# One scheduling region, warm-up matmuls, and row statistics moved from GpSimd to VectorE, in a fused attention, Fourier and feed-forward kernel

## The chip, the cores and the metric

The kernel runs on 1 core of one Trainium2 chip. The metric is device time in microseconds (us) of one execution. The kernel before took 933.96 us, the median of 3 runs (933.89 to 934.87).

## The reference

```python
# q, k, v: (4, 12, 448, 64)    w_ch1: (768, 3072)    w_ch2: (3072, 768)
scores = cap * np.tanh(scale * (q @ k.T) / cap)          # cap = 30
attn = exp(scores - max); attn = attn / (sum(attn) + 1e-9)
x = heads_to_columns(attn @ v)                            # (4, 448, 768)
mixed = np.real(fft(fft(x, axis=1), axis=2))
u = x + mixed
un = (u - mean(u)) / np.sqrt(var(u) + 1e-6)               # over the 768 features
return u + np.maximum(un @ w_ch1, 0) @ w_ch2
```

## The kernel before, in words

Five engines work from one list of steps. A step is a small function (`scores`, `tanh`, `exp`, `weigh`, `normalise`, ...) that issues a few instructions on one or two engines; the table `ORDER` gives every step its place, the list `plan` is sorted by it, and `run` issues it. Each engine takes its instructions strictly in the order in which they were issued to it, and waits at the first whose operands are not ready.

**Attention.** The 12 heads of the 4 batches are 24 pairs of heads; a query block has 84 score tiles. For a tile, TensorE makes the scores (`s`, L378), ScalarE does tanh (L388) and exp (L391) over 900 columns, and TensorE multiplies the weights with the values (`weigh`, tile `av`, L407, 7 units for each pair of heads). The sum `av` of a pair has one PSUM buffer. VectorE divides it by its denominators (`denominators`, L422 and L423; `normalise`, L429) into `u`, and only then can TensorE begin `weigh` of the next pair. The scores have two PSUM buffers.

**Transform of a batch**, once its six pairs are done: folds on VectorE (`fold_tokens` L448, `mirror` L454, `fold_features` L463 to L467), a small matmul (`stage1`, tile `yps`, L479), `combine` (L499), a second matmul (`stage2`, tile `pq`, L507), and its addition to `u` on VectorE (`add_u`, L527 and L531). `moments` (L540, L541) makes mean and variance of each token. `rows` makes from them the inverse deviation `r` by a power and one Newton step, in ten tiny operations of GpSimd (L549 to L558). `rows_cols` and `rows_copy` turn mean and deviation into rows, four small transfers (`rows_out`) put these into DRAM, and `row` reads them back, broadcast to all partitions. `standardise` (L584, VectorE) applies scale and bias to the four blocks of `u` of a batch; `u_cols` (L591, TensorE) transposes them, `u_copy` (ScalarE) takes them to SBUF, `operand` and `operand_rest` (through the helpers L299 on ScalarE and L304 on VectorE) split them into a high and a low part, and `residual` (L715, VectorE) turns the copy back into `u` for the final sum.

**Feed-forward.** w_ch1 and w_ch2 are cut into 12 groups. For each group and batch, `up` (tile `ph`, L725) makes two blocks of 128 hidden units in 36 matmuls of 448 columns, with relu on ScalarE (L736) and the low part on VectorE (L737); `down` (tile `po`, L759) adds 36 matmuls into the output, with an addition on VectorE for every six of them (L767). A `product` step is six of these matmuls. The first group goes in the order U0 D0 U1 D1 U2 D2 U3 D3 (U for `up`, D for `down`, the digit is the batch) and is mixed with the transform of the last batch. The `weights` steps convert weights on VectorE and ScalarE (L638 to L672).

**Two regions.** `run` opens a scheduling region each time that it is called. It is called for the steps up to the last `tanh`, with two double PSUM banks for scores, and again for the rest, with four banks for `up`.

```python
cut = 1 + max(i for i, x in enumerate(plan) if x[2][0] == "tanh")
with tc.tile_pool(name="psum_s", bufs=2, space=PSUM) as stage["scores"]:
    run(plan[:cut])
stage["up"] = ctx.enter_context(tc.tile_pool(name="psum_f", bufs=4, space=PSUM))
run(plan[cut:])
```

At the start, `load_cap` brings `cap`, and `scales` (L325 to L332) makes from it `tscale`, which tanh needs, and then `guard` with an exp on ScalarE, which only the denominators need.

Of the kernel before, what the change touches and what calls it, by code (L numbers as in the profile page):

```python
# [11 lines left out]
F32 = mybir.dt.float32  # L12
# [4 lines left out]
ALU = mybir.AluOpType  # L17
# [86 lines left out]
    "exp": [  # L104
# [4 lines left out]
    ],  # L109
    "fetch": [  # L110
        24, 71, 106, 128, 205, 214, 257, 360, 412, 835, 873, 899, 900, 952
    ],
    "fold_features": [
        211, 212, 193, 202, 419, 438, 402, 405, 641, 648, 630, 642, 822, 825, 820, 821
    ],
    "fold_tokens": [
        67, 68, 163, 137, 187, 200, 261, 345, 397, 401, 399, 394, 456, 463, 627, 636, 626, 633, 673, 684, 806,
        757, 813, 810
    ],
    "load_cap": [  # L120
        4
    ],
    "load_constant": [
        228, 144, 251, 39
    ],
    "load_k": [
        1, 22, 43, 74, 100, 124, 135, 182, 153, 206, 270, 289, 319, 357, 425, 428, 450, 467, 527, 532, 634, 676,
        713, 685
    ],
    "load_q": [  # L130
        2, 10, 12, 42, 69, 50, 95, 73, 107, 127, 174, 157, 183, 242, 244, 274, 262, 312, 342, 366, 370, 395,
        461, 430, 465, 466, 503, 535, 596, 584, 603, 678, 679, 719, 747, 711
    ],
    "load_v": [
        11, 27, 31, 46, 78, 77, 80, 98, 114, 115, 133, 143, 156, 196, 194, 210, 246, 263, 265, 266, 299, 287,
        351, 344, 373, 359, 381, 388, 426, 433, 475, 501, 519, 509, 560, 547, 604, 576, 619, 644, 691, 703, 733,
        731, 759, 741, 784, 782
    ],
    "mirror": [
        188, 201, 400, 404, 628, 639, 814, 817  # L140
    ],
    "moments": [
        283, 295, 302, 306, 482, 498, 508, 510, 727, 729, 755, 728, 853, 855, 856, 854
    ],
    "normalise": [
        47, 65, 104, 126, 162, 184, 209, 255, 286, 315, 341, 390, 435, 455, 495, 536, 567, 592, 640, 672, 722,
        752, 775, 809
    ],
    "operand": [
        643, 384, 574, 416, 474, 523, 646, 777, 647, 723, 689, 824, 807, 818, 880, 913, 919, 915, 941, 940, 924,  # L150
        935, 907, 926
    ],
    "operand_rest": [
        655, 470, 575, 564, 477, 582, 651, 798, 761, 730, 769, 826, 836, 872, 894, 914, 920, 916, 943, 942, 949,
        936, 922, 928
    ],
    "product": [
        811, 812, 827, 828, 829, 841, 848, 851, 852, 861, 862, 863, 864, 865, 871, 875, 879, 885, 901, 908, 909,
        927, 929, 930, 931, 932, 933, 934, 937, 938, 946, 947, 948, 959, 960, 962, 963, 964, 965, 966, 967, 968,
        970, 972, 973, 980, 981, 982  # L160
    ],
    "residual": [
        656, 686, 665, 594, 702, 778, 896, 840, 763, 735, 772, 888, 918, 912, 910, 951, 956, 961, 944, 969, 950,
        974, 945, 953
    ],
    "row": [
        588, 734, 867, 939
    ],
    "rows": [
        327, 545, 768, 870  # L170
    ],
    "rows_cols": [
        343, 563, 779, 876
    ],
    "rows_copy": [
        356, 566, 781, 877
    ],
# [88 lines left out]
def attention_fft_ffn(  # L266
# [53 lines left out]

    def load_cap():
        nc.sync.dma_start(capt, cap.partition_broadcast(P))

    def scales():
        nc.vector.reciprocal(tscale, capt)  # L325
        nc.vector.tensor_scalar_mul(tscale, tscale, 1.0 / math.sqrt(D))


        nc.vector.tensor_scalar_mul(ncap, capt, -1.0)
        nc.vector.tensor_tensor(ncap, ncap, capt, op=ALU.min)  # L330
        nc.scalar.activation(guard, ncap, AF.Exp)
        nc.vector.tensor_scalar_mul(guard, guard, 1e-9)  # L332
# [482 lines left out]
    for i in range(4):  # L815
        at(load_constant, i)
# [173 lines left out]
```

## Time and profile before

| what | value |
|---|---|
| median of 3 runs | 933.96 us |
| the profiled execution's own time | 934.84 us |
| its span, first to last instruction | 932.7 us |
| TensorE busy | 914.1 us (98%) |
| VectorE busy | 715.8 us (77%) |
| ScalarE busy | 326.1 us (35%) |
| GpSimd busy | 16.7 us (2%) |
| TensorE clock granted, mean | 0.998 |

The span is 2.1 us shorter than the execution. In the rows, PE is TensorE's matmuls, PEld its weight loads, DVE is VectorE, ACT ScalarE, POOL GpSimd and SP the queue that issues most transfers. TensorE's busy share is near 98%, so a loss of time on it is seen either as the short idle times in brackets, or as matmuls that take longer than others of the same shape.

### The profile page before, as it was taken

The numbers are of one execution on the slowest core, as the hardware profiler recorded it, in microseconds if no ns is written. First come the engines' busy times: TensorE is split into PE (matmuls) and PEld (weight loads), VectorE is DVE, ScalarE is ACT, GpSimd is POOL, SyncE is SP. The second block draws the span as 40 slices with busy tenths as digits, with TensorE's granted clock in tenths as the row PEclk, the third lists the DMA queues.
The fourth block names the chain that finished last, engine by engine and source line by source line (L and its number), as shares of the span: only waits on it lengthen the run. The fifth ranks groups of instructions, "written<-read, shape, count | busy, mean of one in ns | idle before, by whom it ended". The sixth has DMA issues, their size and how long they took to land.

```text
span 932.7 us, 18658 instructions
## 1 busy us (share of the span) xinstructions
PE 914.1 (98%) x7822; PEld 790.5 (85%) x7822; DVE 715.8 (77%) x1447; ACT 326.1 (35%) x499; POOL 16.7 (2%) x47
## 2 busy tenths in 40 slices
PE   8999999989999999999999999999999999999998
PEld 4666776668889999999998999999999999999997
DVE  2689698879989787878878778777777778777633
ACT  7989989861312222122121221212122221122100
POOL 0001010010100000000000000000000000000000
PEclk9999999999999999999999999999999999999999
DMA  6654435210202121221212121211122111121033
GB/s 184 172 152 134 131 89 130 65 38 1 79 0 85 52 61 51 61 66 54 61 51 61 52 62 47 62 51 51 52 58 62 51 51 51 52 68 51 18 114 123
DMA packets 50611, 66.63 MB, mean 71 GB/s; under 512 B 25568, under 2 KB 36704, under 8 KB 50528
## 3 DMA queue, kind: packets, MB, share of 16 engines
q1 hardware_dynamic: 50240, 65.12, 24.3%
q8 instruction: 61, 1.00, 0.4%
q10 hardware_dynamic: 288, 0.33, 0.1%
q14 instruction: 22, 0.18, 0.1%
HBM read 59.91 MB, written 5.52 MB: 70 GB/s over the span
## 4 chain that ended last, share of the span: by engine, by line
PE 87%; ACT 7%; DVE 4%; issue 1%; POOL 1%; DMA 0%; POOLq 0%; DVEq 0%
PE po L759 37%; PE ph L725 36%; PE av L407 6%; PE s L378 5%; ACT a L391 3%; ACT a L388 3%; PE yps L479 1%; PE pq L507 1%; PE pt L591 1%; DVE xc L715 1%; DVE xc L767 0%; DVE bs L540 0%; DMA q<-qr 0%; POOL ln L551 0%; DVE hh L737 0%
## 5 line engine op out<-in xcount | busy, mean ns | idle before, releaser
L759 PE MATMUL po<-hh,w 128*128 128x448 f32 x1734 | 362.4, 366 | 2.0 <-DVE xc L767 1.6
L725 PE MATMUL ph<-xs,w 128*128 128x448 f32 x1728 | 360.1, 367 | 0.0
L759 PEld LDWEIGHTS po<-hh,w 128*128 128x128 f32 x1734 | 323.1, 188 | 34.0 <-DVE xc L767 4.6
L725 PEld LDWEIGHTS ph<-xs,w 128*128 128x128 f32 x1728 | 324.2, 188 | 28.5 <-issue 0.4
L767 DVE TENSOR_TENSOR xc<-xc,po 128x448 f32<-128x448 f32 x289 | 176.4, 616 | 42.6 <-PE po L759 42.2
L737 DVE SCALAR_TENSOR_TENSOR hh<-ph,hh 128x448 fp32r<-128x448 f32 x96 | 59.9, 624 | 97.0 <-ACT hh L736 96.9
L638 ACT ACTIVATE wt<-raw 128x384 f32<-128x384 f32 x84 | 46.6, 554 | 231.1 <-DVE w L672 231.1
L736 ACT ACTIVATE hh<-ph 128x448 fp32r<-128x448 f32 x96 | 52.3, 545 | 191.8 <-PE ph L725 191.8
L407 PEld LDWEIGHTS av<-vt,a 128*64 128x64 f32 (+3 forms) x3072 | 87.2, 132 | 31.3 <-issue 20.3
L407 PE MATMUL av<-vt,a 128*64 128x65 f32 (+3 forms) x3072 | 93.2, 224 | 4.9 <-issue 4.3
L388 ACT ACTIVATE a<-s,tscale 128x900 f32<-128x900 f32 x84 | 82.7, 1003 | 10.3 <-PE s L378 9.8
L391 ACT ACTIVATE a<-a,capt 128x900 f32<-128x900 f32 x84 | 85.3, 1043 | 1.4
L299 ACT CAST w<-wt 128x384 fp32r<-128x384 f32 x84 | 42.8, 510 | 119.1 <-DVE wt L647 119.1
L378 PE MATMUL s<-q,k 64*64 64x450 f32 x672 | 78.9, 571 | 5.4 <-DMA q<-qr 4.4
L647 DVE SCALAR_TENSOR_TENSOR wt<-wt 128x384 f32<-128x384 f32 x96 | 53.6, 558 | 9.6 <-DVE wt L644 0.5
L644 DVE SCALAR_TENSOR_TENSOR wt<-raw,wt 128x384 uint32<-128x384 uint32 x96 | 53.6, 559 | 3.3
L672 DVE TENSOR_TENSOR w<-wt 128x384 fp32r<-128x384 f32 x96 | 53.6, 558 | 3.3
L666 DVE SCALAR_TENSOR_TENSOR wt<-raw,wt 128x384 f32<-128x384 uint32 x96 | 53.5, 558 | 2.9
L304 DVE TENSOR_TENSOR wt<-wt,w 128x384 f32<-128x384 f32 x96 | 52.8, 550 | 0.0
L378 PEld LDWEIGHTS s<-q,k 64*64 64x64 f32 x672 | 20.6, 136 | 27.2 <-ACT a L388 11.4
L641 DVE TENSOR_SCALAR wt<-raw 128x384 uint32<-128x384 uint32 x96 | 34.1, 355 | 1.1
L663 DVE TENSOR_SCALAR wt<-wt 128x384 uint32<-128x384 uint32 x96 | 34.0, 354 | 0.6
(58 smaller groups left out, 324.0 us busy)
## 6 DMA issues: line engine op xcount, KB each, us to landing
raw<-w2r SPq DMA_DIRECT2D x48, 384.0 KB, 3.9
raw<-w1r SPq DMA_DIRECT2D x48, 384.0 KB, 3.0
q<-qr SPq DMA_DIRECT2D x35, 225.0 KB, 3.9
outT<-xc SPq DMA_DIRECT2D x23, 224.0 KB, 1.9
k<-kr SPq DMA_DIRECT2D x12, 256.0 KB, 3.3
vt<-vr SPq DMA_DIRECT2D x24, 128.0 KB, 4.6
k<-kr SPq DMA_DIRECT2D x12, 192.0 KB, 2.5
vt<-vr SPq DMA_DIRECT2D x24, 96.0 KB, 4.1
```

The source lines that it names most:

```text
L378: nc.tensor.matmul(ps_t[t][h * D : (h + 1) * D, n, :SQ], kt[q, k][rows, k0, h], qk[q, x][rows], start=True, stop=True,)
L388: nc.scalar.activation(a_t[t], ps_t.pop(t)[:, :, :SQ], AF.Tanh, scale=tscale)
L391: nc.scalar.activation(a_t[t], a_t[t], AF.Exp, scale=capt)
L407: nc.tensor.matmul(pa_t[p][q0:q1, j, g * (D + 1) : (g + 1) * (D + 1)], a_t[t][rows, n, OFF[g] + q0 : OFF[g] + q1], vt[rows, p % 2, i], sta ...
L644: nc.vector.scalar_tensor_tensor(tu, hi.bitcast(U32), 0xC0000000, tu, op0=ALU.bitwise_and, op1=ALU.bitwise_or)
L647: nc.vector.scalar_tensor_tensor(t, w, HI_MIN, t, op0=ALU.is_ge, op1=mul)
L666: nc.vector.scalar_tensor_tensor(w, lo, 2.0**-52, w, op0=mul, op1=mul)
L672: nc.vector.tensor_tensor(ws[c][1][:, sl], t, w, op=add)
L725: nc.tensor.matmul(ph[:, :S], w_[:, dc * P : (dc + 1) * P], x_, start=(k_ == 0), stop=(k_ == 3 * NDC - 1),)
L737: nc.vector.scalar_tensor_tensor(hh[:, 1], ph[:, :S], 0.0, f32(hh[:, 0]), op0=ALU.max, op1=sub)
L759: nc.tensor.matmul(po[:, q0:q1], w_[:, dc * P : (dc + 1) * P], hh[:, x_, q0:q1], start=(k_ == 0), stop=(k_ == 3 * GF - 1),)
L767: nc.vector.tensor_tensor(ac[:, q0:q1], ac[:, q0:q1], po[:, q0:q1], op=add)
```

## The change

All steps are issued in one region. Seven matmuls of the identity matrix with itself stand first on TensorE (`warmup`). `scales` now only makes `tscale`; the rest of it is a step of its own (`guards`) behind the second tanh. Of the ten operations of `rows`, the addition and the power stay on GpSimd; six on VectorE take the place of the other eight. The transposed rows come straight from `stat`. `standardise` of the last batch goes to ScalarE. The table has new numbers throughout; two lines of it show their form.

```diff
     "denominators": [
-        45, 64, 97, 123, 161, 178, 208, 254, 284, 314, 335, 389, 434, 454, 494, 530, 565, 591, 638, 670, 715,
-        751, 774, 808
+        50, 65, 98, 124, 162, 186, 211, 255, 289, 314, 342, 383, 434, 456, 502, 539, 564, 596, 639, 671, 727,
+        755, 775, 805
...
+    def warmup():
+        warm = psum.tile([P, 512], F32, tag="d", name="warm")
+        for _ in range(7):
+            nc.tensor.matmul(warm[:, :P], ident, ident, start=True, stop=True)
+
...
     def scales():
         nc.vector.reciprocal(tscale, capt)
         nc.vector.tensor_scalar_mul(tscale, tscale, 1.0 / math.sqrt(D))
+
+    def guards():
...
     def rows(b):
-        ln = line[b] = new([P, 2, 4, 2], F32, "ln", 2, "ln")
-        var = new([P, 4], F32, "var", 1, "var")
+        ln = line[b] = new([P, 4, 2], F32, "ln", 2, "ln")
         t = new([P, 4], F32, "nt", 1, "nt")
-        nc.gpsimd.tensor_copy(ln[:, 0, :, 0], stat[b][:, :, 0])
-        nc.gpsimd.tensor_scalar_add(var, stat[b][:, :, 1], 1e-6)
-        nc.gpsimd.tensor_tensor(ln[:, 1, :, 0], var, mhalf, op=ALU.pow)
-        nc.gpsimd.tensor_tensor(t, ln[:, 1, :, 0], ln[:, 1, :, 0], op=mul)
-        nc.gpsimd.tensor_tensor(t, t, var, op=mul)
-        nc.gpsimd.tensor_scalar(t, t, -0.5, 1.5, op0=mul, op1=add)
-        nc.gpsimd.tensor_tensor(ln[:, 1, :, 0], ln[:, 1, :, 0], t, op=mul)
-        nc.gpsimd.tensor_tensor(ln[:, 0, :, 1], ln[:, 1, :, 0], var, op=mul)
-        nc.gpsimd.tensor_tensor(t, ln[:, 0, :, 0], ln[:, 1, :, 0], op=mul)
-        nc.gpsimd.tensor_scalar_mul(ln[:, 1, :, 1], t, -1.0)
+        n = new([P, 4], F32, "var", 1, "var")
+        mean, var, r = stat[b][:, :, 0], stat[b][:, :, 1], ln[:, :, 0]
+        nc.gpsimd.tensor_scalar_add(t, var, 1e-6)
+        nc.gpsimd.tensor_tensor(r, t, mhalf, op=ALU.pow)
+        nc.vector.tensor_tensor(n, t, r, op=mul)
+        nc.vector.tensor_tensor(n, n, r, op=mul)
+        nc.vector.tensor_scalar(n, n, -0.5, 1.5, op0=mul, op1=add)
+        nc.vector.tensor_tensor(r, r, n, op=mul)
+        nc.vector.scalar_tensor_tensor(ln[:, :, 1], mean, -1.0, r, op0=mul, op1=mul)
+        nc.vector.tensor_tensor(var, t, r, op=mul)
...
-            ps[:8, :R], line[b][:R, 0].rearrange("q g a -> q (g a)"), ident[:R, :R], start=True, stop=True
+            ps[:8, :R], stat[b][:R].rearrange("q g a -> q (g a)"), ident[:R, :R], start=True, stop=True
...
-        scale, bias = ln[:R, 1, g, :1], ln[:R, 1, g, 1:]
-        nc.vector.tensor_scalar(u, u, scale, bias, op0=mul, op1=add)
+        scale, bias = ln[:R, g, :1], ln[:R, g, 1:]
+        if b == B - 1:
+            nc.scalar.activation(u, u, AF.Identity, bias=bias, scale=scale)
+        else:
+            nc.vector.tensor_scalar(u, u, scale, bias, op0=mul, op1=add)
...
     def run(steps):
-        with tc.manual_schedule():
-            for _, _, key, f, args, needs in steps:
...
+        for _, _, key, f, args, needs in steps:
...
-    with tc.tile_pool(name="psum_s", bufs=2, space=PSUM) as stage["scores"]:
-        run(plan[:cut])
-    stage["up"] = ctx.enter_context(tc.tile_pool(name="psum_f", bufs=4, space=PSUM))
-    run(plan[cut:])
+    with tc.manual_schedule():
+        with tc.tile_pool(name="psum_s", bufs=2, space=PSUM) as stage["scores"]:
+            run(plan[:cut])
+        stage["up"] = ctx.enter_context(tc.tile_pool(name="psum_f", bufs=4, space=PSUM))
+        run(plan[cut:])
```

What the changes do to the order of the instructions is shown at three places. Line numbers after the change are 6 to 15 higher than before.

VectorE where pair 22, the last but one, is divided; `den` are the denominators, L584 is `standardise` of batch 2, L448 a fold, `xs` an `operand_rest`, L715 a `residual`. Before:

```order
L541 BN_AGGR stat<-bs 113x2
L448 TENSOR_TENSOR tf<-u 113x4x128
L304 TENSOR_TENSOR xs<-xc,xs 128x448
L715 TENSOR_TENSOR xc<-xc,dev 128x448
L304 TENSOR_TENSOR xs<-xc,xs 128x448 x2
L715 TENSOR_TENSOR xc<-xc,dev 128x448
L584 TENSOR_SCALAR u<-u,ln 113x768 x2
L448 TENSOR_TENSOR tf<-u 113x4x128
L422 TENSOR_SCALAR den<-av,guard 113x8
L423 RECIPROCAL den<-den 113x8
L429 TENSOR_TENSOR u<-av,den 113x4x128
```

and after the change, from the same `moments` on (L554 is the former L541):

```order
L554 BN_AGGR stat<-bs 113x2
L461 TENSOR_TENSOR tf<-u 113x4x128
L310 TENSOR_TENSOR xs<-xc,xs 128x448
L728 TENSOR_TENSOR xc<-xc,dev 128x448
L563 TENSOR_TENSOR var<-nt,ln 128x4
L564 TENSOR_TENSOR var<-var,ln 128x4
L565 TENSOR_SCALAR var<-var 128x4
L566 TENSOR_TENSOR ln<-ln,var 128x4
L567 SCALAR_TENSOR_TENSOR ln<-stat,ln 128x4
L568 TENSOR_TENSOR stat<-nt,ln 128x4
L435 TENSOR_SCALAR den<-av,guard 113x8
L436 RECIPROCAL den<-den 113x8
```

Before, two `standardise`, a fold and two `operand_rest` with a `residual` stand between the `moments` and the denominators of pair 22, although the table has the denominators (774) ahead of both `standardise` (780 and 785) and of one `operand_rest` (798): the two regions had moved four instructions forward. After, they stand behind the division, and the six new tiny operations stand ahead of it.

ScalarE at the start of the program; `guard<-ncap` is the exp of `guards`, L388 (now L401) is tanh, L391 (now L404) is exp. Before:

```order
L311 ACTIVATE guard<-mhalf 128x1
L331 ACTIVATE guard<-ncap 128x1
L388 ACTIVATE a<-s,tscale 128x900 x2
L391 ACTIVATE a<-a,capt 128x900 x2
L388 ACTIVATE a<-s,tscale 128x900
```

After:

```order
L317 ACTIVATE guard<-mhalf 128x1
L401 ACTIVATE a<-s,tscale 128x900 x2
L344 ACTIVATE guard<-ncap 128x1
L404 ACTIVATE a<-a,capt 128x900 x2
L401 ACTIVATE a<-s,tscale 128x900
```

The guard's exp has moved from ahead of the first two tanh to behind them.

VectorE in the transform of the last batch; L527 and L531 (now L540 and L544) are the additions of `stage2`, each group of four belonging to one product in PSUM, and L767 (now L780) is the addition behind a `down` product. Before:

```order
L737 SCALAR_TENSOR_TENSOR hh<-ph,hh 128x448
L527 TENSOR_TENSOR u<-u,pq 113x2x384 x4
L531 TENSOR_TENSOR u<-u,pq 113x384 x4
L767 TENSOR_TENSOR xc<-xc,po 128x448
L531 TENSOR_TENSOR u<-u,pq 113x384 x4
L767 TENSOR_TENSOR xc<-xc,po 128x448 x2
```

After:

```order
L750 SCALAR_TENSOR_TENSOR hh<-ph,hh 128x448
L540 TENSOR_TENSOR u<-u,pq 113x2x384 x4
L544 TENSOR_TENSOR u<-u,pq 113x384 x8
L780 TENSOR_TENSOR xc<-xc,po 128x448 x2
L550 MEMSET stat 128x8
```

The `down` product that stood between the third and the fourth `stage2` now follows the fourth.

## Rows read from the trace of the kernel before

**Rows 1.** The page's first part: busy time and share by engine.
```profile
PE 914.1 (98%) x7822; PEld 790.5 (85%) x7822; DVE 715.8 (77%) x1447; ACT 326.1 (35%) x499; POOL 16.7 (2%) x47
```

**Rows 2.** Stages: length; busy us of PE, PEld, DVE, ACT, POOL; clock; DMA share, GB/s.
```profile
10.00:60.00 50.00, 49.00 (x1149) 31.31 (x1143) 30.81 (x71) 49.38 (x53) 0.00 (x0) 1.00 0.62 175
60.00:187.00 127.00, 125.00 (x2726) 89.05 (x2724) 106.94 (x237) 112.44 (x138) 7.74 (x20) 1.00 0.40 109
187.00:204.00 17.00, 12.91 (x306) 10.31 (x301) 11.34 (x25) 10.41 (x14) 4.15 (x10) 0.90 0.15 39
204.00:282.00 78.00, 73.98 (x460) 64.27 (x459) 72.21 (x149) 18.72 (x40) 4.06 (x10) 1.00 0.10 28
282.00:932.00 650.00, 647.64 (x3174) 593.97 (x3172) 493.02 (x960) 130.31 (x254) 0.00 (x0) 1.00 0.20 60
```

**Rows 3.** Timeline, 0 to 9 us: start, duration, engine, line, operation, idle before.
```profile
4.43 6.24 PE L378 MATMUL s<-q,k 64*64 64x450 f32 x32 [4.43 <-DMA q<-qr]
5.89 0.15 DVE L326 TENSOR_SCALAR tscale<-tscale 128x1 f32<-128x1 f32 x1
6.39 0.20 ACT L331 ACTIVATE guard<-ncap 128x1 f32<-128x1 f32 x1 [3.73 <-DVE ncap L330]
6.50 0.99 ACT L388 ACTIVATE a<-s,tscale 128x900 f32<-128x900 f32 x1
7.78 1.01 ACT L388 ACTIVATE a<-s,tscale 128x900 f32<-128x900 f32 x1 [0.28 <-PE s L378]
```

**Rows 4.** Score matmuls as a group, 0 to 14, then 140 to 190 us.
```profile
L378 PE MATMUL s<-q,k 64*64 64x450 f32 x40 | 7.2, 872 | 4.4 <-DMA q<-qr 4.4
...
L378 PE MATMUL s<-q,k 64*64 64x450 f32 x176 | 19.9, 552 | 0.0
```

**Rows 5.** Stages of 1 us, columns as in rows 2.
```profile
5.00:6.00 1.00, 1.00 (x11) 0.25 (x6) 0.28 (x3) 0.00 (x0) 0.00 (x0) 1.00 0.80 232
...
200.00:201.00 1.00, 1.00 (x24) 1.00 (x23) 0.00 (x0) 0.00 (x0) 0.00 (x0) 0.50 0.47 56
```

**Rows 6.** Timeline, 188 to 204 us, around the division of pair 22.
```profile
188.97 3.63 PE L407 MATMUL av<-vt,a 128*64 128x65 f32 x128
189.57 0.21 DVE L541 BATCH_NORM_AGGREGATE stat<-bs 113x2 f32<-113x12 f32 x1
191.03 1.39 POOL L551 TENSOR_TENSOR ln<-var,mhalf 128x4 f32<-128x4 f32 x1
192.71 0.62 DVE L715 TENSOR_TENSOR xc<-xc,dev 128x448 f32<-128x448 f32 x1
194.74 1.27 DVE L584 TENSOR_SCALAR u<-u,ln 113x768 f32<-113x768 f32 x2 [1.41 <-POOL ln L558]
196.53 0.22 DVE L422 TENSOR_SCALAR den<-av,guard 113x8 f32<-113x8 f32 x1
197.02 0.69 DVE L429 TENSOR_TENSOR u<-av,den 113x512 f32<-113x512 f32 x1
197.81 5.17 PE L407 MATMUL av<-vt,a 64*64 64x65 f32 x128 [3.17 <-issue]
203.03 0.23 DVE L422 TENSOR_SCALAR den<-av,guard 113x8 f32<-113x8 f32 x1 [3.44 <-PE av L407]
```

**Rows 7.** Timeline, 210 to 224 us, transform of the last batch on TensorE.
```profile
210.83 1.78 PE L479 MATMUL yps<-seqT,ff 112*64 112x113 f32 x32
...
216.42 2.18 PE L507 MATMUL pq<-featT,y 97*64 97x192 f32 x32
...
220.73 1.48 PE L759 MATMUL po<-hh,w 128*128 128x448 f32 x6
222.14 1.20 PE L507 MATMUL pq<-featT,y 97*64 97x192 f32 x16
```

**Rows 8.** VectorE's groups by shape, whole span: busy us, mean ns of one.
```profile
L527 DVE TENSOR_TENSOR u<-u,pq 113x768 f32<-113x768 f32 x16 | 14.3, 942 | 0.7 <-PE pq L507 0.7
L584 DVE TENSOR_SCALAR u<-u,ln 113x768 f32<-113x768 f32 x16 | 10.1, 671 | 2.1 <-POOL ln L558 2.0
L423 DVE RECIPROCAL den<-den 113x8 f32<-113x8 f32 x24 | 4.9, 203 | 0.8
```

More of the change, by code (lines that the diff above doesn't have):

```diff
@@ L115 @@
     ],
     "fold_tokens": [
-        67, 68, 163, 137, 187, 200, 261, 345, 397, 401, 399, 394, 456, 463, 627, 636, 626, 633, 673, 684, 806,
-        757, 813, 810
+        67, 68, 167, 137, 191, 204, 257, 347, 392, 401, 393, 391, 459, 470, 630, 641, 598, 600, 674, 691, 804,
+        763, 808, 809
+    ],
+    "guards": [
+        11
     ],
     "load_cap": [
-        4
+        5
     ],
     "load_constant": [
-        228, 144, 251, 39
+        233, 139, 217, 116
     ],
     "load_k": [
-        1, 22, 43, 74, 100, 124, 135, 182, 153, 206, 270, 289, 319, 357, 425, 428, 450, 467, 527, 532, 634, 676,
@@ L128 @@
-        713, 685
+        2, 30, 42, 75, 100, 90, 144, 184, 168, 213, 270, 320, 285, 366, 423, 428, 455, 469, 530, 546, 612, 678,
+        634, 720
     ],
     "load_q": [
-        2, 10, 12, 42, 69, 50, 95, 73, 107, 127, 174, 157, 183, 242, 244, 274, 262, 312, 342, 366, 370, 395,
-        461, 430, 465, 466, 503, 535, 596, 584, 603, 678, 679, 719, 747, 711
+        5, 13, 11, 44, 70, 71, 95, 112, 99, 141, 152, 161, 185, 245, 250, 265, 311, 316, 344, 368, 373, 386,
+        464, 426, 468, 467, 520, 552, 604, 571, 644, 637, 681, 723, 749, 717
@@ L138 @@
+        703, 759, 741, 779, 782
     ],
     "mirror": [
-        188, 201, 400, 404, 628, 639, 814, 817
+        197, 215, 396, 402, 631, 642, 810, 812
     ],
     "moments": [
-        283, 295, 302, 306, 482, 498, 508, 510, 727, 729, 755, 728, 853, 855, 856, 854
+        263, 266, 300, 303, 495, 498, 533, 517, 735, 739, 757, 736, 854, 858, 856, 859
     ],
     "normalise": [
-        47, 65, 104, 126, 162, 184, 209, 255, 286, 315, 341, 390, 435, 455, 495, 536, 567, 592, 640, 672, 722,
-        752, 775, 809
+        51, 66, 104, 125, 163, 187, 212, 256, 290, 315, 346, 388, 439, 458, 504, 540, 565, 597, 643, 672, 729,
@@ L148 @@
+        756, 780, 806
     ],
     "operand": [
-        643, 384, 574, 416, 474, 523, 646, 777, 647, 723, 689, 824, 807, 818, 880, 913, 919, 915, 941, 940, 924,
-        935, 907, 926
+        650, 407, 578, 415, 476, 521, 638, 837, 648, 728, 692, 820, 829, 823, 833, 916, 917, 921, 944, 896, 912,
+        924, 936, 955
     ],
     "operand_rest": [
-        655, 470, 575, 564, 477, 582, 651, 798, 761, 730, 769, 826, 836, 872, 894, 914, 920, 916, 943, 942, 949,
-        936, 922, 928
+        658, 473, 579, 417, 479, 587, 687, 840, 764, 737, 781, 821, 862, 863, 926, 920, 923, 925, 947, 946, 913,
@@ L161 @@
+        973, 975, 976, 982, 983, 984
     ],
     "residual": [
-        656, 686, 665, 594, 702, 778, 896, 840, 763, 735, 772, 888, 918, 912, 910, 951, 956, 961, 944, 969, 950,
-        974, 945, 953
+        661, 686, 682, 616, 721, 830, 891, 864, 765, 738, 783, 902, 918, 875, 928, 945, 930, 957, 954, 948, 953,
+        981, 959, 966
     ],
     "row": [
-        588, 734, 867, 939
+        594, 734, 874, 911
     ],
     "rows": [
-        327, 545, 768, 870
+        329, 550, 768, 865
     ],
@@ L172 @@
     "rows_cols": [
-        343, 563, 779, 876
+        345, 569, 785, 877
     ],
     "rows_copy": [
-        356, 566, 781, 877
+        359, 577, 786, 878
     ],
     "rows_out": [
-        380, 424, 504, 555, 602, 697, 698, 732, 794, 795, 859, 860, 897, 898, 902, 903
+        385, 430, 453, 528, 603, 702, 731, 733, 788, 811, 818, 872, 880, 885, 904, 905
     ],
     "scales": [
-        5
+        6
     ],
     "scores": [
[4 rows of a table removed]
[4 rows of a table added]
     ],
     "stage1": [
-        229, 237, 225, 243, 440, 432, 458, 462, 659, 669, 657, 671, 834, 837, 830, 832
+        231, 241, 228, 246, 441, 433, 461, 462, 662, 675, 659, 679, 836, 839, 832, 835
@@ L207 @@
-        895, 904, 911
+        378, 379, 400, 404, 419, 421, 573, 580, 607, 593, 628, 627, 801, 802, 822, 824, 857, 873, 892, 894, 897,
+        898, 908, 914
     ],
     "u_copy": [
-        382, 383, 408, 414, 422, 423, 573, 579, 620, 621, 629, 635, 804, 805, 816, 823, 858, 881, 889, 890, 893,
-        905, 906, 923
+        381, 395, 405, 406, 425, 429, 574, 595, 618, 622, 633, 640, 803, 819, 825, 827, 861, 886, 893, 895, 899,
+        900, 910, 915
+    ],
+    "warmup": [
+        0
     ],
@@ L811, in convert @@
                 at(weights, 3 * i + n, needs=[("fetch", i)] + ([("weights", 3 * i + n - 1)] if i + n else []))
+    at(warmup)
     at(load_cap)
     at(scales, needs=[("load_cap",)])
+    at(guards, needs=[("scales",)])
     for i in range(4):
@@ L840, in attend @@
             if 7 * p + 6 in (2 * t, 2 * t + 1):
-                at(denominators, p, needs=[("weigh", 7 * p + 6)] + ([("denominators", p - 1)] if p else []))
+                at(denominators, p, needs=[("weigh", 7 * p + 6), ("guards",)] + ([("denominators", p - 1)] if p else []))
                 at(normalise, p, needs=[("denominators", p)])
@@ L932, in run @@
     def run(steps):
-        with tc.manual_schedule():
-            for _, _, key, f, args, needs in steps:
-                for n in needs:
-                    assert n in done, (key, n)
-                f(*args)
-                done.add(key)
-    cut = 1 + max(i for i, x in enumerate(plan) if x[2][0] == "tanh")
-    with tc.tile_pool(name="psum_s", bufs=2, space=PSUM) as stage["scores"]:
-        run(plan[:cut])
-    stage["up"] = ctx.enter_context(tc.tile_pool(name="psum_f", bufs=4, space=PSUM))
-    run(plan[cut:])
+        for _, _, key, f, args, needs in steps:
+            for n in needs:
+                assert n in done, (key, n)
+            f(*args)
+            done.add(key)
+    cut = 1 + max(i for i, x in enumerate(plan) if x[2][0] == "tanh")
+    with tc.manual_schedule():
[3 more added lines that the diff above has]
+        run(plan[cut:])
 def kernel(q, k, v, cap, moe_w_ch1, moe_w_ch2):
```

28 lines of the change are left out of this document (13 added, 15 removed), and 40 rows, old and new, of the table ORDER.

## The prediction

> **What bounds the kernel now.** I read the busy shares first: TensorE 98%, VectorE 77%, ScalarE 35% [rows 1]. That names TensorE, but the shares are means over stages, so the table by stage comes second [rows 2]. From 282 us to the end TensorE is busy 647.64 of 650 us and nothing is late; these 650 us hold only products, the same before and after, so whatever the change is worth must be won before 282. There the reader sees four different stages. From 10 to 60 us ScalarE is busy 49.38 of 50: tanh and exp set the pace. From 60 to 187 TensorE is busy 125.0 of 127. From 187 to 204 it is busy only 12.91 of 17, and the granted clock is 0.90. From 204 to 282 it is busy 73.98 of 78 while VectorE is busy 72.21: both are near their limit.
>
> Third, the timeline of the weak stage [rows 6]. TensorE finishes the weights of pair 22 at 188.97 + 3.63 = 192.6, and starts pair 23 only at 197.81, because `av` has one buffer and VectorE must divide first. VectorE could have begun at 193.3, behind the residual of 192.71, but next in its queue stand two `standardise` of batch 2. They wait for GpSimd until 194.74 (1.41 us idle), then take their own time with a fold behind them, and the division runs from 196.53 to 197.02 + 0.69 = 197.7. The same 128 matmul records that took 3.63 us for pair 22 then take 5.17 for pair 23, and a stretch of 1 us in the middle shows a granted clock of 0.50 [rows 5], the 1.2 GHz level: it fell after TensorE had stood nearly still since 193. VectorE in turn idles 3.44 us for these matmuls and begins the last division at 203.03.
>
> **The change part by part.**
>
> *One region and the row operations (one term, since both act on the division of pair 22).* In the new order three long operations follow the last `moments`, then the six tiny ones, then the division; the `standardise`, a fold and the operands come after. From the aggregate's end at 189.57 + 0.21 = 189.8 [rows 6], three operations that start about 0.6 us apart (the residual's 0.62) bring VectorE to 191.5. GpSimd had a copy and an addition before its power, which began at 191.03, 1.25 us after the aggregate; with the copy gone I halve that, so the power of 1.39 us ends near 191.8, and VectorE waits 0.3 us for it. The six tiny operations are not in the trace. The nearest rows are 0.15 us (128x1) [rows 3] and 0.203 (113x8) [rows 8] below, and the residual's 0.62 above, were they as slow as long ones; they depend on each other, so I take 0.22 each, 1.3 us, with 0.9 and 3.7 for the range. So the division starts at 193.2 and takes 197.7 - 196.53 = 1.2, and pair 23 starts at 194.5 in place of 197.81. TensorE has the scores of the last tile in between, so it stands still for about 1 us instead of 4, and I expect the clock to stay up: 3.63 us, end at 198.1. VectorE still has two operations of 0.6, four `standardise` (1.27 us for two, so 2.5), a copy and a fold, 4.5 us in all from 194.4, and begins the last division at 198.9 in place of 203.03: **-4.1 us**. The last fold, features and `stage1` hang on this one, and TensorE's first products fill the time until then as before. Bounds: with slow tiny operations and a fallen clock 2.4 + 1.5 are lost of it, which leaves -0.2; with no wait left at all the idle 3.17 and the slow 1.54 on TensorE plus a microsecond of the wait for the rows go, -5.7.
>
> The Trainium skill ("VectorE: DVE Perf Modes", section "The TRN2 errata — SBUF-src ops pay a fixed extra latency per instruction") speaks against moving tiny work to VectorE: every instruction pays a fixed latency whatever its size. Its formula for an fp32 two-input operation gives an estimate of 0.16 us for four elements, 1.0 us for six; by it the term would be -4.4.
>
> *VectorE's work from there to 282 us.* In the new order it has, between the last division and the end of the fourth `down`, four `standardise` fewer (4 x 0.671 = -2.7 [rows 8]), six tiny operations more (+1.3), and one `operand_rest` and one `residual` that used to stand ahead of the division (2 x 0.6 = +1.2). Since VectorE is 93% busy here I count it in full: **-0.2 us**; 0 and -0.4 if half or double of it reaches the path. The four `standardise` on ScalarE cost nothing: it is busy 18.72 of 78 us there [rows 2], and a 768-wide one is estimated at 0.85 us from the 0.99 of a 900-wide tanh [rows 3]. What waits behind them on ScalarE are a copy and a relu; TensorE has eight products (1.2 us each) queued for that time.
>
> *The order of `stage2` in the last batch.* Before, it ran from 216.42 to 222.14 + 1.20 = 223.3 with a product of 1.48 inside, so 5.4 us net [rows 7]. Now all four stand together on two PSUM buffers: two take 2.2 us, the third waits for two additions of 0.942 [rows 8] behind the first, the fourth for two more; the fourth ends 6.0 us after the first begins: **+0.5 us** (0 to +1).
>
> *Start of the program.* The first tanh starts at 6.50, behind the guard's exp of 6.39; the second at 7.78, having waited 0.28 us for scores [rows 3]. `tscale` is ready at 6.04. In the first 14 us a score matmul takes 872 ns on average, later 552 [rows 4], while the granted clock reads 1.00 from the first microsecond [rows 5]. If the warm-up matmuls, which need only the identity and fill the 4.43 us that TensorE waits for q, take this slow stretch upon them, the first tanh starts at 6.1 and the second at 7.1; the guard's exp (0.20) comes behind them, and the first exp is 0.4 to 0.5 us earlier. From there to 60 us ScalarE is the limit, so this stays: **-0.4 us**. If they buy nothing, the second tanh stays at 7.78 and the guard's exp is added behind it: +0.2. The best case is -0.7.
>
> The Trainium skill ("TensorE: Matmul & The Clock Gate", section "Part 1: The HAM clock gate (the "warmup" mystery)") says that the array begins at half rate and gets the full one only once it has been kept busy. By it the slow first scores are a cold array, and the term is -0.4; by the clock row alone, which reads full, it would be +0.2. The 872 against 552 ns side with the page.
>
> *All else.* The new table moves nearly every step between 10 and 187 us by a few places. At the changes of pair the same or more TensorE work covers the division, in the order, so I cost it at nothing, +-1.5 us; the six tiny operations of batches 0 and 1 lie beside 127 - 106.94 = 20 us of idle VectorE [rows 2].
>
> Sum: -4.1 - 0.2 + 0.5 - 0.4 = -4.2 us against the profiled execution of 934.84 us (span 932.7 and 2.1 around it), so 930.6. The median of the runs shown is 0.9 lower, 933.96, and from it 929.7 follows, which is my forecast.
>
> **Rivals.**
>
> *More than the sum.* TensorE idles 2.0 us from 60 to 187 and 4.0 from 204 to 282 [rows 2]. If the new table also takes half of these, 3.0 more: 926.7. For it: in several places the order puts one score tile more between two pairs. Against: at others one fewer.
>
> *The stall only shrinks.* The tiny operations stand in front of the division and wait for GpSimd's power; if that still keeps TensorE still long enough for the clock to fall, the 1.5 us of slow matmuls come back: 931.2. For it: the fall came after an idle time of which 1 us remains. Against: 1 us is a quarter of it.
>
> *Given back later.* If VectorE's list from 204 to 282 is what ends there and has no slack (5.8 us idle in the rows), TensorE arrives 4 us earlier and waits more: only the start's 0.4 and about as much again remain, 933.2. Against: VectorE's own last division also comes 4.1 us earlier.
>
> *Slower: VectorE becomes the limit from 60 us on.* Place: the rows of batches 0 and 1, where twelve tiny operations (2.6 us) are added and VectorE waits in order for GpSimd's addition and power twice (2 x 2.0, from 0.6 and 1.39). If all of it delays the divisions, 6.6 us are lost and the result is 929.7 + 6.6 = 936.3. It decides only if the 20 us of idle VectorE there are none of them at the right place; weight conversions stand between `moments` and the tiny operations as cover, so it is unlikely.
>
> **How the numbers follow.** The forecast gets 0.62, and its own range is 928.2 to 931.0; the bigger gain 0.12; the clock 0.13; given back 0.08; slower 0.05. A difference under 0.2% (1.9 us) can't be told from none: faster means below 932.1, slower above 935.8. So faster is 0.62 + 0.12 + 0.13 = 0.87, the same 0.08, slower 0.05. The range leaves out half of the bigger gain, and the two last cases, 0.19 together: 926.8 to 932.4.
>
> **What would show it.** Right: pair 23's matmuls start within 2 us of the end of pair 22's, last about 3.7 us, with no 0.50 in the clock; the last division starts near 199; the second tanh near 7.1 us; the stage from 282 on is shifted as a whole. Wrong: a clock of 0.50 after pair 22; tiny operations of more than 0.4 us; the first products at 204 as before; or TensorE idle between 200 and 280 grown from 4 to 8 us.

## The result, and the profile after

The changed kernel takes 926.32 us, the median of 4 runs (925.67 to 928.0), against 934.26 (933.89 to 934.87) for the kernel before on the same chip: a ratio of 0.9917, 95% interval 0.9901 to 0.9933. That is 8 us faster, where 4.2 were forecast, and half a microsecond below the range. The profiled execution took 926.14 us, its span is 924.2, so 8.5 us are gone from the span of 932.7. The busy times on the page after, to be read beside [rows 1]:

```profile
PE 913.0 (99%) x7836; PEld 790.8 (86%) x7836; DVE 717.1 (78%) x1467; ACT 327.8 (35%) x503; POOL 6.8 (1%) x15
```

The stages, with the columns of [rows 2]; the last begins and ends 8 us earlier than there, so the one before it is 8 us shorter:

```profile
10.00:60.00 50.00, 49.66 (x1176) 32.54 (x1176) 32.14 (x74) 48.50 (x52) 0.00 (x0) 1.00 0.69 197
60.00:187.00 127.00, 125.84 (x2732) 88.21 (x2729) 110.50 (x253) 115.02 (x141) 2.67 (x4) 1.00 0.39 106
187.00:204.00 17.00, 16.61 (x321) 14.58 (x318) 16.18 (x39) 10.39 (x16) 1.74 (x2) 1.00 0.01 2
204.00:274.00 70.00, 65.50 (x405) 56.83 (x401) 64.27 (x139) 18.82 (x36) 1.67 (x2) 1.00 0.12 36
274.00:924.00 650.00, 647.12 (x3177) 594.24 (x3175) 492.92 (x960) 130.34 (x253) 0.00 (x0) 1.00 0.21 60
```

The weak stage from 187 to 204 us is weak no more: TensorE 16.61 of 17 instead of 12.91, clock 1.00 instead of 0.90. But the two stages ahead of it have changed as well: TensorE stands still for 0.34 instead of 1.00 us from 10 to 60, and for 1.16 instead of 2.0 from 60 to 187. The timeline around the division of pair 22, to be read beside [rows 6]:

```profile
186.44 3.63 PE L420 MATMUL av<-vt,a 128*64 128x65 f32 x128
187.05 0.21 DVE L554 BATCH_NORM_AGGREGATE stat<-bs 113x2 f32<-113x12 f32 x1
187.99 1.26 POOL L562 TENSOR_TENSOR ln<-nt,mhalf 128x4 f32<-128x4 f32 x1
189.28 0.16 DVE L563 TENSOR_TENSOR var<-nt,ln 128x4 f32<-128x4 f32 x1 [0.27 <-POOL ln L562]
190.23 0.22 DVE L435 TENSOR_SCALAR den<-av,guard 113x8 f32<-113x8 f32 x1
190.72 0.69 DVE L442 TENSOR_TENSOR u<-av,den 113x512 f32<-113x512 f32 x1
191.52 3.63 PE L420 MATMUL av<-vt,a 64*64 64x65 f32 x128 [0.39 <-PE rt L573]
195.67 0.21 DVE L435 TENSOR_SCALAR den<-av,guard 113x8 f32<-113x8 f32 x1
```

Pair 22's matmuls start at 186.44 in place of 188.97, which is 2.53 us earlier; pair 23's follow with 0.39 us of idle time in place of 3.17 and last 3.63 us in place of 5.17. The last division starts at 195.67 in place of 203.03, 7.36 us earlier. So the gain has three parts: 2.53 us ahead of pair 22, 4.83 between pair 22's start and the last division, and 8.5 - 7.36 = 1.1 behind it.

The 2.53 us are not of one place. The reciprocals of pairs 6, 9 and 21; ahead of each, the same number of matmuls of every kind (the warm-up aside) stands on TensorE in both orders. Before:

```profile
56.29 0.20 DVE L423 RECIPROCAL den<-den 113x8 f32<-113x8 f32 x1
84.86 0.20 DVE L423 RECIPROCAL den<-den 113x8 f32<-113x8 f32 x1
187.68 0.20 DVE L423 RECIPROCAL den<-den 113x8 f32<-113x8 f32 x1
```

After:

```profile
55.25 0.20 DVE L436 RECIPROCAL den<-den 113x8 f32<-113x8 f32 x1
83.04 0.20 DVE L436 RECIPROCAL den<-den 113x8 f32<-113x8 f32 x1
185.16 0.20 DVE L436 RECIPROCAL den<-den 113x8 f32<-113x8 f32 x1
```

They come 1.0, 1.8 and 2.5 us earlier: the lead grows bit by bit. It was not won at the first tanh. The start of the program after (PEld are weight loads of TensorE; four scores follow each group of four):

```profile
1.35 3.35 PE L330 MATMUL warm<-ident 128*128 128x128 f32 x14 [1.35 <-POOL ident masks.py:199]
5.44 0.24 PEld L391 LDWEIGHTS s<-q,k 64*64 64x64 f32 x4 [0.50 <-issue]
6.19 0.25 PEld L391 LDWEIGHTS s<-q,k 64*64 64x64 f32 x4 [0.51 <-issue]
6.48 1.01 ACT L401 ACTIVATE a<-s,tscale 128x900 f32<-128x900 f32 x1 [3.82 <-PE s L391]
7.76 1.01 ACT L401 ACTIVATE a<-s,tscale 128x900 f32<-128x900 f32 x1 [0.28 <-PE s L391]
```

In this execution the first scores still take 0.75 us for four, and the tanh start at 6.48 and 7.76, against 6.50 and 7.78 [rows 3].

### The profile page after: what moved, and what is told of

It reads as the page before. It is cut to its first block, busy times and chain, and to the rows that moved or that the text cites. A ratio compares the mean times of both kernels' runs of the same rounds, so it can differ in the third digit from the quotient of the medians.

```text
span 924.2 us, 18681 instructions
## 1 busy us (share of the span) xinstructions
PE 913.0 (99%) x7836; PEld 790.8 (86%) x7836; DVE 717.1 (78%) x1467; ACT 327.8 (35%) x503; POOL 6.8 (1%) x15
## 4 chain that ended last, share of the span: by engine, by line
PE 92%; DVE 4%; ACT 2%; issue 1%; POOL 0%; DVEq 0%; POOLq 0%; ACTq 0%
PE po L772 38%; PE ph L738 37%; PE av L420 8%; PE s L391 7%; PE pq L520 1%; PE yps L492 1%; PE pt L604 1%; ACT a L404 1%; ACT a L401 1%; DVE u L540 0%; DVE u L544 0%; ACT u L595 0%; PE warm L330 0%; DVE tf L461 0%; DVE u L442 0%
## 5 line engine op out<-in xcount | busy, mean ns | idle before, releaser
L772 PE MATMUL po<-hh,w 128*128 128x448 f32 x1734 | 362.0, 366 | 1.7 <-DVE xc L780 1.1
L738 PE MATMUL ph<-xs,w 128*128 128x448 f32 x1728 | 359.0, 366 | 0.0
L780 DVE TENSOR_TENSOR xc<-xc,po 128x448 f32<-128x448 f32 x289 | 176.4, 616 | 41.6 <-PE po L772 41.3
L420 PEld LDWEIGHTS av<-vt,a 128*49 128x49 f32 (+3 forms) x3072 | 85.0, 130 | 28.4 <-issue 14.6
L420 PE MATMUL av<-vt,a 128*49 128x65 f32 (+3 forms) x3072 | 91.0, 222 | 1.5 <-issue 0.8
L401 ACT ACTIVATE a<-s,tscale 128x900 f32<-128x900 f32 x84 | 82.7, 1008 | 13.2 <-PE s L391 12.8
L404 ACT ACTIVATE a<-a,capt 128x900 f32<-128x900 f32 x84 | 85.7, 1046 | 0.9
L391 PE MATMUL s<-q,k 64*64 64x450 f32 x672 | 77.6, 561 | 0.6 <-ACT a L401 0.5
L391 PEld LDWEIGHTS s<-q,k 64*64 64x64 f32 x672 | 20.1, 134 | 21.7 <-ACT a L401 9.5
```

The lines of the kernel that those rows point to most:

```text
L391: nc.tensor.matmul(ps_t[t][h * D : (h + 1) * D, n, :SQ], kt[q, k][rows, k0, h], qk[q, x][rows], start=True, stop=True,)
L401: nc.scalar.activation(a_t[t], ps_t.pop(t)[:, :, :SQ], AF.Tanh, scale=tscale)
L404: nc.scalar.activation(a_t[t], a_t[t], AF.Exp, scale=capt)
L420: nc.tensor.matmul(pa_t[p][q0:q1, j, g * (D + 1) : (g + 1) * (D + 1)], a_t[t][rows, n, OFF[g] + q0 : OFF[g] + q1], vt[rows, p % 2, i], sta ...
L738: nc.tensor.matmul(ph[:, :S], w_[:, dc * P : (dc + 1) * P], x_, start=(k_ == 0), stop=(k_ == 3 * NDC - 1),)
L772: nc.tensor.matmul(po[:, q0:q1], w_[:, dc * P : (dc + 1) * P], hh[:, x_, q0:q1], start=(k_ == 0), stop=(k_ == 3 * GF - 1),)
```

## The experiments

What had to be settled: where the 2.53 us come from, whether the region or the row operations made the early division, and what the other edits are worth. Each kernel was timed in five rounds beside the kernel before; its ratio goes with its own runs of that kernel (medians of 933.8 to 934.3).

| kernel | median, us | ratio to before, 95% interval |
|---|---|---|
| the changed kernel | 926.32 | 0.9917 (0.9901 to 0.9933) |
| the same again | 925.95 | 0.9912 (0.9899 to 0.9926) |
| before, one region | 929.02 | 0.9948 (0.9934 to 0.9961) |
| old code, one region, new order | 931.66 | 0.9978 (0.9968 to 0.9988) |
| new code, old order | 931.69 | 0.9974 (0.9965 to 0.9983) |
| changed, two regions | 929.42 | 0.9949 (0.9937 to 0.9962) |
| changed, no warm-up | 925.55 | 0.9909 (0.9895 to 0.9923) |
| changed, rows on GpSimd | 927.35 | 0.9932 (0.9920 to 0.9944) |
| changed, `standardise` on VectorE | 931.45 | 0.9970 (0.9961 to 0.9979) |
| changed, old order to pair 6 | 926.75 | 0.9924 (0.9912 to 0.9936) |
| changed, one product moved | 925.25 | 0.9905 (0.9892 to 0.9919) |
| changed, three products moved | 927.66 | 0.9932 (0.9919 to 0.9946) |

**One region alone.**

```diff
-    def run(steps):
-        with tc.manual_schedule():
+    with tc.manual_schedule():
```

The new line stands around both calls of `run`.

> The kernel before, with the two scheduling regions made one and nothing else changed. In the order this puts four operations of VectorE (one operand, two `standardise`, one fold) behind the division of pair 22 instead of ahead of it. Theory A (two separate gains: the division of pair 22 through the region, about 4 us, and the new order of steps ahead of it, about 2.5 to 3 us; warm-up, guards, row operations and the ScalarE `standardise` close to nothing): 930.0 us, -4, with pair 23's matmuls starting within 2 us of the end of pair 22's, and pair 22's matmuls starting at 189.0 as before. Theory B (the upstream gain comes from the edited code, warm-up, guard and row operations, and not from the order): the same 930 here. Theory C (the row operations off GpSimd, not the region, bring the early division): 933.5, within 1 us of before.

929.02 us, 5.2 less than before. Its denominators of pairs 22 and 23, on VectorE:

```profile
192.62 0.23 DVE L422 TENSOR_SCALAR den<-av,guard 113x8 f32<-113x8 f32 x1
...
198.44 0.21 DVE L422 TENSOR_SCALAR den<-av,guard 113x8 f32<-113x8 f32 x1
```

These are 3.9 and 4.6 us earlier than in [rows 6], with all ten row operations on GpSimd. Pair 21's reciprocal starts at 187.63, as before (187.68). Theory C falls: the region makes the early division, and it changes nothing ahead of it.

**New order, old code.** The table of the change in the kernel above (`guards` and `warmup` do not exist in it).

> The code of the kernel before (no warm-up, guard with the scales, ten row operations on GpSimd, all `standardise` on VectorE) in one region, with the new order of steps. Theory A: 927.2 us, -7, and pair 22's matmuls start at about 186.5 instead of 188.97. Theory B: 930, the same as the one region alone, and pair 22's matmuls start near 189. Theory C: 931 (new order gives its 2.5, division of pair 22 still late).

Pair 21's reciprocal starts at 184.95 and the last division's at 195.85 (185.16 and 195.91 in the changed kernel): all of the 2.5 us is the order's, none needs the new code, so theory B falls. Two of TensorE's waits before 187 us in the kernel before (us in all, times, longest; for those put down to "issue" the profile names no cause), and the first two stages with the new order:

```profile
PE av L407 <- issue: 1.1, 2, 0.6
PE s L378 <- ACT a L388: 0.8, 2, 0.5
```

```profile
10.00:60.00 50.00, 49.85 (x1182) 32.77 (x1176) 32.15 (x73) 48.60 (x52) 0.00 (x0) 1.00 0.67 196
60.00:187.00 127.00, 126.33 (x2742) 88.73 (x2739) 109.13 (x244) 115.19 (x141) 7.60 (x20) 1.00 0.39 106
```

Scores no longer wait for tanh, and ahead of the weights 0.3 us of the 1.1 are left. Of 3.0 us of idle time in these stages [rows 2], 0.8 remain (0.15 and 0.67). But the time is 931.66, not 927.2. TensorE's waits from 60 to 282 us have a new one:

```profile
PE pt L597 <- DVE u L590: 3.1, 1, 3.1
```

`u_cols` of the last batch wait for a `standardise`. Theory A had missed this: the new order needs one of the edits.

**Old order, new code.**

> The changed kernel's code (warm-up, guard by itself, eight row operations on VectorE, last `standardise` on ScalarE, one region) with the old order of steps, the warm-up first and the guard behind the second tanh. Theory A: 930.0 us, -4, and pair 22's matmuls start within 0.5 us of 189.0. Theory B: 927, and pair 22's matmuls start near 186.5. Theory C: 930, with this order the row operations are early enough.

Upstream theory A holds: pair 21's reciprocal starts at 188.00. But 931.69, which no theory expected, is 2.7 worse than the one region alone. VectorE and TensorE at pair 22, and a wait further on (in us, times, longest):

```profile
192.12 0.16 DVE L563 TENSOR_TENSOR var<-nt,ln 128x4 f32<-128x4 f32 x1 [0.27 <-POOL ln L562]
194.26 0.22 DVE L435 TENSOR_SCALAR den<-av,guard 113x8 f32<-113x8 f32 x1
195.54 3.63 PE L420 MATMUL av<-vt,a 64*64 64x65 f32 x128 [1.58 <-issue]
```

```profile
PE pt L604 <- ACT u L595: 1.1, 2, 0.6
```

In the old order the six tiny operations and two long ones stand ahead of the division, which comes 1.64 us later than with one region alone; and `u_cols` wait for ScalarE's `standardise`. So neither half of the change does without the other: with the old code the new order costs 2.6 us over the one region alone, with the old order the new code costs 2.7, and both together save 2.7.

**Two regions again.** The changed kernel with the region opened in `run`.

> The changed kernel with the two scheduling regions of before. In the order, two `standardise` and a fold move ahead of the division of pair 22 on VectorE, and the last exp and tanh change places on ScalarE. Theory A: the division comes some 2 to 3 us later and TensorE stands still long enough for the granted clock to fall again, 929.3 us, +3 against the changed kernel. Theory B: the same, 929.3. Theory C: 926.3, no change, since the row operations decide.

929.42, 3.1 slower, as A and B expected. VectorE, TensorE, and a stage of 1 us:

```profile
189.06 1.27 DVE L597 TENSOR_SCALAR u<-u,ln 113x768 f32<-113x768 f32 x2
190.85 0.22 DVE L435 TENSOR_SCALAR den<-av,guard 113x8 f32<-113x8 f32 x1
192.14 5.21 PE L420 MATMUL av<-vt,a 64*64 64x65 f32 x128 [2.22 <-issue]
```

```profile
194.00:195.00 1.00, 1.00 (x24) 1.00 (x22) 0.58 (x1) 0.00 (x0) 0.00 (x0) 0.50 0.07 17
```

After 2.22 us without a matmul the granted clock falls to the 1.2 GHz level, and the 1.6 us of slow matmuls are back.

**No warm-up.** `at(warmup)` is left out.

> The changed kernel without its seven warm-up matmuls, all else the same. Theory A (what the start gains is small and half of it is absorbed on the way): 926.8 us, +0.5; the first scores take 0.75 us for four records until about 9 us, and the division of pair 21 comes 0.2 to 0.5 us later than the changed kernel's 185.16. Rival B (the warm-up brings the whole gain ahead of 187 us): 928.9, +2.6, with the division of pair 21 at about 187.7.

925.55 us, pair 21's reciprocal at 184.58. Theory B falls again. A's half microsecond is not seen in the time either, and pair 21 is divided 0.58 us earlier than in the changed kernel, not later. The last experiment shows part of the reason.

**Row operations on GpSimd.** The ten lines of the old `rows`, and its operand of `rows_cols`, in the changed kernel.

> The changed kernel with the ten row operations back on GpSimd in their old form; the last batch's `standardise` stays on ScalarE. Theory A (the row operations hardly matter once one region has put the division ahead of the `standardise`): 926.8 us, +0.5, with the division of pair 22 within 0.5 us of 190.49. Rival C (the loss of about 5 us that the old code has with the new order after 209 us is the row operations'): 930 to 931.

927.35, +1.0, between the theories but next to A. Pair 22's reciprocal starts at 189.31, 1.2 us ahead of the 190.49 that A gave, because pair 21's is 1.1 us early here (184.06). From pair 21's reciprocal to the last it takes 10.73 us, against 10.75 in the changed kernel, so the row operations on VectorE gain nothing there. In the profiled execution the granted clock then falls during `stage2`, of which more below.

**`standardise` on VectorE.**

```diff
-        if b == B - 1:
+        if False:
             nc.scalar.activation(u, u, AF.Identity, bias=bias, scale=scale)
```

> The changed kernel with the last batch's four `standardise` on VectorE instead of ScalarE. Theory A (this edit is what the new order needs: the fourth `standardise` stands behind weight conversions on VectorE, TensorE stands still for 3 us near 232 to 235 and the granted clock falls): 930.5 us, +4.2, with a granted clock of 0.50 between 235 and 243. Rival C (row operations are what the new order needs): 926.8, +0.5.

931.45, +5.1, where A expected +4.2. The wait of TensorE, what stands on VectorE, and stages of 1 us:

```profile
PE pt L604 <- DVE u L597: 3.3, 2, 3.1
```

```profile
230.44 1.84 DVE L597 TENSOR_SCALAR u<-u,ln 113x768 f32<-113x768 f32 x3
...
235.10 0.67 DVE L597 TENSOR_SCALAR u<-u,ln 113x768 f32<-113x768 f32 x1
```

```profile
233.00:234.00 1.00, 0.00 (x0) 0.00 (x0) 0.96 (x3) 0.00 (x0) 0.00 (x0) 1.00 0.34 132
...
236.00:237.00 1.00, 1.00 (x6) 0.78 (x7) 1.00 (x3) 0.53 (x1) 0.00 (x0) 0.50 0.00 0
```

Between the third and the fourth `standardise` stand six operations of weight conversion; TensorE has nothing until the fourth is done, and then runs at the lower clock beyond 240. This accounts for what the old code lost with the new order, 5.3 us against the changed kernel.

**Old order up to pair 6**, then the new one, with the new code.

> The changed kernel with the old order of steps up to the division of pair 6 (about 56 us) and the new order for all that is left. Theory A (the gain of the new order ahead of 187 us is spread: about 0.9 us to pair 6, 0.8 to pair 9, 1.0 from pair 17 to 21): 927.2 us, +0.9, and the division of pair 21 near 186.0. Rival D (it all comes from the stage that ScalarE paces): 928.9, +2.6. Rival E (it all comes later): 926.3.

926.75, and the reciprocal of pair 21 at 185.71, 0.55 later than in the changed kernel. D falls; A's 0.9 is a little high, and the time cannot tell it from E's zero. So about 0.6 us of the 2.5 hangs on the order before 56 us, although the lead there is already 1.0; the rest hangs on the order behind it.

**Products into the waits of the last batch.** In the changed kernel TensorE waits for VectorE's additions between its `stage2`:

```profile
209.04 2.18 PE L520 MATMUL pq<-featT,y 97*64 97x192 f32 x32
212.23 1.19 PE L520 MATMUL pq<-featT,y 97*64 97x192 f32 x16 [1.02 <-DVE u L540]
213.96 1.19 PE L520 MATMUL pq<-featT,y 97*64 97x192 f32 x16 [0.54 <-DVE u L540]
...
218.12 1.49 PE L772 MATMUL po<-hh,w 128*128 128x448 f32 x6 [0.33 <-DVE xc L780]
```

Place 852 of `product` became 847.5 in one kernel; in the other 843, 852 and 853 became 835.5, 843.5 and 847.5.

> The changed kernel with one product of six matmuls (a `down` that stands behind the last batch's `stage2`) moved between its second and third `stage2`, nothing else. Theory A (the waits of 1.02 and 0.54 us in the last `stage2` are lost time on TensorE, and a clock fall after them costs 2 us more in some executions): 925.3 us, -1.0 against the changed kernel, no wait over 0.6 us there and a granted clock of 1.00 from 204 to 240. Rival F (VectorE's additions are what ends there, and a product only pushes the third `stage2` back): 926.3.

> The changed kernel with three products moved into the waits of the last batch: the last piece of `up` between the second and third `stage1`, one `down` ahead of `stage2`, one between its second and third. Theory A: the waits of 1.04, 1.02 and 0.54 us are filled, 924.3 us, -2.0 against the changed kernel. Rival F (VectorE's `combine` and additions are what ends there): 926 to 926.5, with new waits of a microsecond at the head of `stage2`.

One product moved, same columns:

```profile
209.97 1.49 PE L777 MATMUL po<-hh,w 128*128 128x448 f32 x6
211.39 1.20 PE L525 MATMUL pq<-featT,y 97*64 97x192 f32 x16
212.79 1.19 PE L525 MATMUL pq<-featT,y 97*64 97x192 f32 x16 [0.20 <-DVE u L545]
215.18 2.67 PE L777 MATMUL po<-hh,w 128*128 128x448 f32 x12 [1.20 <-DVE u L549]
```

925.25 us is the lowest median of all, but its interval overlaps that of the changed kernel (925.95 on the same chip). The waits of 1.02, 0.54 and 0.33 became 0.20, and a new one of 1.20 came behind the fourth `stage2`: of 1.89 us, 0.49 was won there. A's time came true, but its waits did not go; and in the profiled execution pair 21's reciprocal starts at 184.00, 1.2 us earlier than in the changed kernel, so most of the difference lies ahead of the moved product. Three products moved are worse, 927.66: the fourth `stage1` waits 1.36 and a product 1.02 us. F is right about what ends there: VectorE.

**The changed kernel again**, for the warm-up.

> The changed kernel as it is, on the same chip as the two before, with another profile. Theory A (the warm-up brings the first exp from 8.8 to about 7.9 us in most executions, and 0.4 to 0.6 of that is left at the division of pair 21): 926.3 us, the division of pair 21 at 184.0 to 184.6 where the first exp starts before 8.0, at about 185.2 where it starts near 8.8. Rival G (the warm-up is worth nothing behind the first pairs): pair 21 at 185.2 whatever the first exp does.

925.95 us; first exp at 8.61, pair 21 at 185.02. Three more start rows, of the kernel with the rows on GpSimd, show what the warm-up can do:

```profile
5.07 0.15 PEld L391 LDWEIGHTS s<-q,k 64*64 64x64 f32 x4 [0.22 <-issue]
5.45 0.15 PEld L391 LDWEIGHTS s<-q,k 64*64 64x64 f32 x4 [0.22 <-issue]
7.92 1.98 ACT L404 ACTIVATE a<-a,capt 128x900 f32<-128x900 f32 x2
```

Here four scores take 0.38 us and the first exp starts 0.85 earlier than in the changed kernel. Of nine profiles with the warm-up, six reach this pace before 6 us, and three (two of them of the changed kernel itself) keep the half pace past 6.19. With the new order throughout, a first exp between 7.90 and 8.28 goes with pair 21 at 183.95 to 184.25 (five profiles); one between 8.61 and 8.78, with or without warm-up, with 184.58 to 185.16 (four). So G falls: an early first exp, by 0.7 us on average, goes with an early pair 21, by 0.85. But no median shows it. The changed kernel was profiled twice and kept the half pace both times, against A's "most executions"; whether the kernel or the single execution decides this is not shown. With the old order it did not arrive: there the first exp is at 8.19 and pair 21 at 188.00. The later place of the guard's exp was not tried by itself.

## Why the prediction was right in direction and too small

*Failed: "All else ... I cost it at nothing".* This is the step. The new order took 2.5 us ahead of pair 22, more than the 1.5 left to this term, and the kernel with the new order and the old code shows that the order alone does it. The reason given, that the same or more TensorE work covers each division, looked at the changes of pair alone; scores that wait for tanh (0.8 us) are not seen there. The rows for it were in the table by stage: TensorE's idle time of 1.0 and 2.0 us from 10 to 60 and 60 to 187 [rows 2]. Of these 3.0 us, 0.8 are left with the new order and the old code, 1.5 in the changed kernel (0.34 and 1.16) and 0.9 in the one without warm-up (50 - 49.43 = 0.57 and 127 - 126.67 = 0.33). In the changed kernel matmuls are also busy for less time: up to pair 21's reciprocal the scores 75.3 us in place of 76.6 and the weights 83.8 in place of 84.4. Why these are shorter stays open. The prediction had read the first as the price of ScalarE's limit and put half of the second into the rival "More than the sum". That rival gave 926.7 and was the nearest, but it expected the gain from 204 to 282 too, where the idle time did not shrink: 4.0 us before, 4.5 after.

*The division of pair 22: right, somewhat small.* -4.1 forecast, -4.83 measured, with every sign named: pair 23's matmuls within 2 us of pair 22's (5.08 - 3.63 = 1.45), 3.63 us long, no clock of 0.50. Of the parts, the wait for the power was 0.27 (0.3 forecast), and the six tiny operations take 0.95 us from 189.28 to the denominators (1.3 forecast). The Trainium skill ("VectorE: DVE Perf Modes", section "The TRN2 errata — SBUF-src ops pay a fixed extra latency per instruction") gave an estimate of 0.16 us for each and -4.4 for the term. The rows, 0.16, agree with it, and it was nearer than the middle between my neighbouring rows. What the prediction had wrong is the credit: it made one term of the region and the row operations. One region alone moves the last division by 4.6 us, the row operations gain nothing (10.73 us with them on GpSimd, 10.75 on VectorE, from pair 21 to the last), and in the old order they stand ahead of a later division.

*"The four `standardise` on ScalarE cost nothing": true and beside the point.* It was costed as 2.7 us less on a busy VectorE, of which the net -0.2 came into the sum; each takes 1.02 us on ScalarE, where 0.85 was estimated. Undone by itself it costs 5.1 us, because the new order has weight conversions between the third and the fourth. The prediction never asked what the new order would do without this edit.

*The start: mechanism right, not reliable.* -0.4 forecast; nothing in the two profiles of the changed kernel (first exp at 8.77 and 8.61, before at 8.69), 0.4 to 0.8 us in six of the nine with warm-up (7.90 to 8.28). The Trainium skill ("TensorE: Matmul & The Clock Gate", section "Part 1: The HAM clock gate (the "warmup" mystery)") says that the array starts at half rate until it has been kept busy. The six profiles agree. In the other three the same 14 records of warm-up did not end the half pace in time for the first tanh. In all of them the granted clock reads 1.00, so that row cannot tell the two apart.

*The order of `stage2`: right.* +0.5 forecast; TensorE's waits at `pq` grew from 1.0 to 1.6 in the last batch. One product moved into the gap wins back 0.5 us, three lose more than that, as the two kernels with moved products show.

*Behind the last division* 1.1 us more are gone, where +0.3 was forecast. About 0.5 of it is on TensorE already when the last pair ends (202.98 before, 195.15 after, 7.83 earlier). The rest is in no wait: the sum of busy time over the same 3462 products is lower, 362.0 + 359.0 = 721.0 in place of 362.4 + 360.1 = 722.5. Why they are shorter was not tried and stays open.

*The other rivals.* The stall does not only shrink: 0.39 us are left and the clock stays. Nothing is given back later. VectorE does not become the limit from 60 us on: there TensorE is busier than before, 125.84 of 127 us.

## What to carry to other kernels

A table that moves nearly every step is not worth nothing because each move is small: add up the idle time of the bounding engine over all stages that it touches, and keep that sum as a term with its own middle, not as a margin. When an order and several code edits come together, ask for each edit what the new order does without it; here, beside one region alone, order and code each lost 2.6 to 2.7 us by themselves and gained 2.7 together. Where the bounding engine stalls, look whether its clock falls behind the stall: after 3.17 us the slow matmuls cost 1.54 more, after 2.22 they cost 1.58.

## What was not expected of the hardware

A fall of the granted clock needs no single long wait. In the kernel with the rows on GpSimd, and in the one with the old order to pair 6, the profiled execution has the waits of about 1.0 and 0.5 us between `stage2` and then about 6.5 and 3 us at 0.50, the 1.2 GHz level. A stage of 1 us of the first:

```profile
218.00:219.00 1.00, 1.00 (x4) 0.87 (x4) 0.21 (x1) 0.00 (x0) 0.00 (x0) 0.50 0.00 0
```

The changed kernel, with the same waits of 1.02 and 0.54 us, kept 1.00 in both of its profiles, but its execution of 928.0 us, the longest, has a mean clock of 0.996. With the rows on GpSimd, three executions with a mean of 0.999 or 1.000 took 926.7 to 927.4 us and two at 0.996 took 929.0 and 929.2. So such a fall goes with about 2 us, more than the waits ahead of it, and comes in some executions only; that these two waits bring it about is read from the two profiles and was not tried. It does not explain every long execution: with the old order to pair 6 the longest, 928.62 us, has a mean clock of 1.00. In the kernel with one product moved, with waits of 0.20 and 1.20 us there, the four executions lie within 0.7 us (924.9 to 925.6), too few to show that the fall is gone.
